# Gate and value products of a gated unit: seven block products per batch in place of full products, with input sums kept in DRAM

## The chip, the cores and the metric

The kernel runs on one core of a Trainium2 chip. The metric is the device time of one execution in microseconds. Before the change, three runs gave a median of 2069.04 us (2067.13 to 2071.77). The execution that the profiler recorded took 2068.53 us; the span from its first to its last instruction is 2066.6 us.

## The reference

Three layers follow each other. A retention layer (4 batches, 8 heads, 576 positions, head width 64) gives x with 2304 tokens and 512 features. A gated unit with 1536 hidden features and then eight dense experts follow:

```python
# gated unit
rms = np.sqrt(np.mean(x * x, axis=-1, keepdims=True) + 1e-06)
xn = x / rms * rms_g
g = xn @ w_gate                      # (2304, 512) @ (512, 1536)
silu = g * (1.0 / (1.0 + np.exp(-g)))
val = xn @ w_val                     # (2304, 512) @ (512, 1536)
x = silu * val @ w_out               # (2304, 1536) @ (1536, 512)
# experts: P is (2304, 8), from x @ w_gate by eight rounds of row and column scaling
for e in range(8):
    out += P[:, e:e+1] * (np.maximum(x @ w1[e], 0) @ w2[e])
```

## The kernel before

Everything is computed in float32 by splitting each operand into a high half (`hi`, rounded to fp32r) and a low half (`lo`, the rest). A product is three matmuls: hi by hi, hi by lo, lo by hi (lines 174 to 176, `products`). Tokens are the moving columns, features lie on the 128 partitions.

The gated unit takes its 1536 hidden features in six sweeps (`NSWEEP`) of two blocks of 128 (`SWEEP`). A sweep goes over all 2304 tokens. The first sweep runs inside the retention stage, in eight blocks of 288 tokens, as soon as a batch of 576 tokens is normed. Sweeps two to six run in the five blocks of

```python
BLOCKS = [(0, 512), (512, 512), (1024, 512), (1536, 384), (1920, 384)]
```

In `gated_block` (line 179 on) a block of a sweep needs, for each of its two m: a gate product `gv` of four k blocks by three matmuls, a value product of the same size, the silu on ScalarE (line 196), the multiplication on VectorE (line 202), and the split of the result into `ghi` (ScalarE, line 203) and `glo` (VectorE, line 204). Then four output products `x` of six matmuls each follow, and VectorE adds each of them to `acc` in SBUF (line 225). Products go to four rotating PSUM banks for `gv` and four for `x`. A block has 72 matmuls, a sweep 360.

The weights come from DRAM as 64-bit words, 512 KB for a block of 128 hidden features of one matrix. They are narrowed to float32 by GpSimd (lines 122 and 130), VectorE (lines 123, 124, 126) and ScalarE (line 127), and split by ScalarE (line 142) and VectorE (line 144). `step_weights` moves these chains on by one step at a time, at places written into the loop, so all engines follow one fixed program order; each engine works its own queue in that order.

The experts behind it already use a seven-block scheme: `block_product` (line 775) takes x and w1 as two by two blocks and needs seven products instead of eight; products run into the single PSUM banks px, py, pz and pv, and ScalarE copies px to py and py to pz to start the next product from a sum (lines 870 and 889). Its first pair of features is `n = 0`.

Every DMA that the change touches goes through the queue of SP, in program order.

Of the kernel before, what the change touches and what calls it, by code (L numbers as in the profile page):

```python
# [23 lines left out]
E = 8  # L24
# [7 lines left out]
BLOCKS = [(0, 512), (512, 512), (1024, 512), (1536, 384), (1920, 384)]  # L32
# [6 lines left out]
PAD = 320  # L39
T = 384  # L40
UNIT = 2 * T
NU = NT // UNIT
# [8 lines left out]
def retention_glu_experts(ctx: ExitStack, tc: tile.TileContext, a, out):  # L51
# [15 lines left out]
    wpool = glu.enter_context(tc.tile_pool(name="wpool", bufs=1, side="right"))  # L67
# [20 lines left out]
    for s in range(NSWEEP):  # L88
        for m in range(s * SWEEP, (s + 1) * SWEEP):
            sources += [a["gate"][m], a["val"][m]]  # L90
        sources += [a["wout"][m] for m in range(s * SWEEP, (s + 1) * SWEEP)]
    raw, raw_of, pieces, slot_of, active = {}, {}, {}, {}, {}
    wslots = wpool.tile([128, NW, 2, 512], F32R, name="wslots")
    pad = wpool.tile([128, PAD // 2], mybir.dt.bfloat16, name="pad")
    slots = [[(wslots[:, i, 0, :], wslots[:, i, 1, :]) for i in range(NW)], []]
    raw_slots = list(range(NRAW))
    n_load, n_next, n_slot, n_done = [0], [0], [0], [0]
# [14 lines left out]
    def narrow_weights(i):  # L112


# [4 lines left out]
        x_f, sign = cv[:, 0, :], cv[:, 1, :]  # L119
        x = x_f.bitcast(I32)  # L120
        least = float(np.array((1023 - 126) << 20, np.int32).view(np.float32))
        nc.gpsimd.tensor_scalar(sign, high_f, -least, None, ALU.is_le)  # L122
        nc.vector.tensor_scalar(x, low, 29, 1 << 30, ALU.logical_shift_right, ALU.bitwise_xor)
        nc.vector.scalar_tensor_tensor(x, high, 3, x, ALU.logical_shift_left, ALU.bitwise_xor)
        yield
        nc.vector.scalar_tensor_tensor(sign, high_f, least, sign, ALU.is_ge, ALU.subtract)
        nc.scalar.activation(x_f, x_f, AF.Abs)
        free_raw(i)
        yield
        nc.gpsimd.tensor_mul(x_f, x_f, sign)  # L130
        yield
        return x_f

    def prepare(i):
        x = yield from narrow_weights(i)
        free = slots[i // (3 * SWEEP) in (2, 4)]
        while i != n_slot[0] or not free:
            yield
        n_slot[0] += 1
        hi, lo = pieces_of = free.pop(0)  # L140
        slot_of[i] = free, pieces_of
# [4 lines left out]

    def step_weights(load=True):
        for i in sorted(active):
            if next(active[i], True):
                del active[i]  # L150
        i = n_next[0]
        if i in raw and len(active) < NCONV:
            active[i] = prepare(i)
            next(active[i])
            n_next[0] += 1
        if load:
            load_weights()
# [6 lines left out]
    def done(n):  # L164
        for _ in range(n):
# [13 lines left out]
    def gated_block(s, t0, n, last, pmm, pac, hp, tp, together, w):  # L179
        p0 = s * 3 * SWEEP  # L180
        g = []
        for m in range(SWEEP):
# [15 lines left out]
            if last:  # L198
                done(2)
# [488 lines left out]
    for _ in first_unit:  # L688
        pass
# [622 lines left out]
```

## Time and profile before

| what | value |
|---|---|
| median of three runs | 2069.04 us |
| profiled execution, its span | 2068.53 us, 2066.6 us |
| first sweep and retention | up to 213 us |
| sweep two | 213 to 296 us |
| sweeps three, four, five | 74.09, 74.09 and 73.99 us |
| sweep six | 518 to about 598 us |
| experts, prepared while their weights are read | 598 to about 1120 us |
| experts, with the weights kept | about 1120 us to the end |
| granted clock over the span | 0.992 |

A row of the profile names the line of the kernel, the engine, the operation, the tile written and the tiles read. PE is the matmul engine, DVE VectorE, ACT ScalarE, POOL GpSimd, SP the queue that issues most DMAs. Matmuls overlap at their ends in the record, so the price of one is read from start to start and not from its duration.

### The profile page before, as it was taken

How to read it: one execution, taken by the hardware profiler on the slowest of the kernel's cores; microseconds unless marked ns; L12 is line 12 of the kernel's file. 1: busy time of each engine (PE TensorE's matmuls, PEld its weight loads, DVE VectorE, ACT ScalarE, POOL GpSimd, SP SyncE). 2: the span in 40 equal slices, each digit the busy share in tenths (PEclk: the TensorE clock that was granted, in tenths of full speed). 3: DMA queues.
4: the chain of work that ended last, by engine and by line, in shares of the span. 5: the costliest groups of instructions: out<-in, count | busy, mean ns of one | idle time of the engine just before them, and what ended most of it. 6: DMA issues, size and time to landing. Idle time of an engine off the chain costs nothing.

```text
span 2066.6 us, 30376 instructions
## 1 busy us (share of the span) xinstructions
PE 2035.1 (98%) x11526; PEld 1883.8 (91%) x11526; DVE 1482.2 (72%) x2324; ACT 862.9 (42%) x1655; POOL 842.9 (41%) x746
## 2 busy tenths in 40 slices
PE   8999999999999999999999999999999999999998
PEld 5688788899788989999998999999999999999998
DVE  6764775653468887777776777777788677777777
ACT  3443331221254454444444544444445544444443
POOL 4411442310024454544561545444455454544443
PEclk8899999999999999999999999999999999999999
DMA  7420221100028888888878767676766676767673
GB/s 233 156 90 1 69 75 41 62 29 3 0 96 306 296 297 299 309 300 306 306 285 329 262 252 275 244 268 247 280 246 260 251 273 252 260 251 281 241 282 138
DMA packets 112690, 436.58 MB, mean 211 GB/s; under 512 B 12297, under 2 KB 30473, under 8 KB 96161
## 3 DMA queue, kind: packets, MB, share of 16 engines
q1 hardware_dynamic: 110048, 432.72, 57.4%
q8 instruction: 90, 1.47, 0.3%
q10 hardware_dynamic: 2496, 1.94, 0.3%
q14 instruction: 56, 0.45, 0.1%
HBM read 312.40 MB, written 122.21 MB: 210 GB/s over the span
## 4 chain that ended last, share of the span: by engine, by line
PE 89%; DVE 6%; ACT 2%; issue 1%; POOL 1%; DMA 1%; ACTq 0%; SPq 0%; DVEq 0%; POOLq 0%
PE pz L775 9%; PE py L775 9%; PE px L775 9%; PE qx L1006 6%; PE qy L1006 6%; PE qz L1006 6%; PE gv L174 5%; PE gv L175 4%; PE gv L176 4%; PE y L175 4%; PE y L176 4%; PE y L174 4%; PE qz L775 3%; PE x L174 2%; PE x L175 2%; PE x L176 2%
## 5 line engine op out<-in xcount | busy, mean ns | idle before, releaser
L1183 POOL TENSOR_TENSOR acc<-z,a_block 128x384 f32<-128x384 f32 x63 | 64.0, 1016 | 446.5 <-DVE z L1177 446.5
L775 PE MATMUL py<-sx,w1s 128*128 128x384 f32 x1152 | 233.0, 336 | 2.8 <-ACT py L1099 2.5
L775 PEld LDWEIGHTS py<-sx,w1s 128*128 128x128 f32 x1152 | 203.5, 188 | 7.2 <-ACT py L1099 4.3
L775 PE MATMUL px<-xhi,w1s 128*128 128x384 f32 x640 | 188.5, 335 | 0.0
L996 ACT CAST xhi<-acc 128x384 fp32r<-128x384 f32 x316 | 156.0, 514 | 69.6 <-POOL acc L1183 35.4
L1000 DVE TENSOR_TENSOR xlo<-acc,xhi 128x384 fp32r<-128x384 f32 x191 | 177.5, 956 | 1.8 <-ACT xhi L996 1.8
L1000 POOL TENSOR_TENSOR xlo<-acc,xhi 128x384 fp32r<-128x384 f32 x125 | 145.4, 1163 | 32.2 <-ACT xhi L996 32.2
L1014 DVE TENSOR_TENSOR acc<-acc,qz 128x384 f32<-128x384 f32 x246 | 134.9, 548 | 26.0 <-PE qz L1006 26.0
L577 POOL TENSOR_TENSOR t<-rw 128x256 f32<-128x256 f32 x32 | 43.0, 1343 | 234.6 <-issue 126.9
L122 POOL TENSOR_SCALAR cv<-raw 128x512 f32<-128x512 f32 x36 | 63.1, 1757 | 182.6 <-DVE wslots L144 91.6
L175 PE MATMUL gv<-xlo,wslots 128*128 128x512 f32 (+2 forms) x368 | 127.4, 346 | 3.0 <-DVE xlo L408 1.7
L174 PE MATMUL gv<-xhi,wslots 128*128 128x512 f32 (+2 forms) x368 | 128.5, 349 | 0.4 <-ACT xhi L405 0.4
L176 PE MATMUL gv<-xhi,wslots 128*128 128x512 f32 (+2 forms) x368 | 126.9, 345 | 0.0
L202 DVE TENSOR_TENSOR t<-t,gv 128x512 f32<-128x512 f32 (+2 forms) x66 | 38.8, 589 | 115.8 <-PE gv L176 115.7
L775 PEld LDWEIGHTS px<-xhi,w1s 128*128 128x128 f32 x640 | 117.9, 188 | 0.3
L1014 DVE TENSOR_TENSOR acc<-acc,qx 128x384 f32<-128x384 f32 x123 | 67.4, 548 | 70.1 <-PE qx L1006 70.1
L775 PE MATMUL pz<-xhi,w1s 128*128 128x384 f32 x384 | 113.8, 337 | 3.2 <-DVE z L930 2.3
L775 PE MATMUL pz<-sx,w1s 128*128 128x384 f32 x576 | 115.6, 335 | 0.0
L775 PE MATMUL px<-xlo,w1s 128*128 128x384 f32 x320 | 106.9, 334 | 0.0
L820 DVE SCALAR_TENSOR_TENSOR acc<-y,prob,acc 128x512 f32<-128x512 f32 x144 | 101.4, 742 | 6.1 <-PE y L176 6.1
L176 PE MATMUL y<-xlo,xhi 128*128 128x512 f32 x264 | 103.9, 393 | 0.0
L175 PE MATMUL y<-xlo,xhi 128*128 128x512 f32 x264 | 103.7, 393 | 0.0
(379 smaller groups left out, 6037.4 us busy)
## 6 DMA issues: line engine op xcount, KB each, us to landing
w1s<-w_kept SPq DMA_DIRECT2D x64, 1792.0 KB, 7.1
w_kept<-w1s SPq DMA_DIRECT2D x32, 1792.0 KB, 6.6
rw<-in_w_dram SPq DMA_DIRECT2D x64, 512.0 KB, 5.5
w_kept<-xlo SPq DMA_DIRECT2D x64, 512.0 KB, 3.7
w2s<-w_kept SPq DMA_DIRECT2D x32, 1024.0 KB, 6.9
w_extra<-w_kept SPq DMA_DIRECT2D x32, 768.0 KB, 7.6
w_kept<-xlo SPq DMA_DIRECT2D x44, 384.0 KB, 4.1
w2c<-w_kept SPq DMA_DIRECT2D x32, 512.0 KB, 7.7
```

Source lines behind the costliest of these rows:

```text
L122: nc.gpsimd.tensor_scalar(sign, high_f, -least, None, ALU.is_le)
L174: nc.tensor.matmul(ps, lhsT=lh, rhs=rh, start=start, stop=False)
L175: nc.tensor.matmul(ps, lhsT=lh, rhs=rl, start=False, stop=False)
L176: nc.tensor.matmul(ps, lhsT=ll, rhs=rh, start=False, stop=stop)
L577: nc.gpsimd.tensor_sub(t[:, 0, :], w[:, 3, :], w[:, 0, :])
L775: nc.tensor.matmul(ps, lhsT=l, rhs=r[:, k, :], start=start and k == 0 and i == 0, stop=k == 1 and i == 2, skip_group_check=True,)
L820: nc.vector.scalar_tensor_tensor(o, y_2, pe, o, ALU.mult, ALU.add)
L996: nc.scalar.copy(hi, x)
L1000: (engine or nc.vector).tensor_sub(lo, x, f32(hi))
L1006: nc.tensor.matmul(ps, lhsT=l, rhs=r, start=start and i == 0, stop=i == 2, skip_group_check=True)
L1014: nc.vector.tensor_add(dst, dst, ps)
L1183: nc.gpsimd.tensor_add(sums[0], z[:, 0, :], h_blocks[0])
```

## The change

For sweeps two to six, gate and value products use the seven-block scheme with batches of 576 tokens as two halves of 288 columns, and 512 features as two halves of 256. The weights of a sweep (two blocks of 128 hidden features) give seven blocks of 256 by 128: four of the original ones and combinations of them, made on GpSimd by four subtractions of 256 columns for each pair of raw blocks. The sums of x (S1 to S4) are made on GpSimd when a batch is normed, split, and stored to DRAM (`x_kept`). S1 is later loaded over the part of `xhi` and `xlo` that is needed no more; S2, S3 and S4 of each batch are loaded again in every sweep into a ring of four places. A unit is one batch in one sweep: a gate half, then a value half, each of seven block products of six matmuls. Between them stand the eight output products (six matmuls of 288 columns each) of the unit before.

The core of the diff:

```diff
-BLOCKS = [(0, 512), (512, 512), (1024, 512), (1536, 384), (1920, 384)]
+HB = S // 2
@@ narrowing, now also for pairs of blocks
+    def pair_of_blocks(at, idx):
...
+        nc.gpsimd.tensor_sub(t0[:, :256], b12, b11)
+        nc.gpsimd.tensor_sub(t0[:, 256:], b22, b12)
+        yield
+        nc.gpsimd.tensor_sub(t1[:, :256], b22, t0[:, :256])
+        nc.gpsimd.tensor_sub(t1[:, 256:], b21, t1[:, :256])
...
+                nc.scalar.copy(r[:, 0, p, :], x)
...
+                nc.vector.tensor_sub(r[:, 1, p, :], x, f32(r[:, 0, p, :]))
@@ after the norm of a batch
+        nc.gpsimd.tensor_add(s1, a21, a22)
+        nc.gpsimd.tensor_sub(s2, s1, a11)
+        nc.gpsimd.tensor_sub(s3, a11, a21)
+        nc.gpsimd.tensor_sub(s4, a12, s2)
+    def split_sums(b, sums):
+        for i, t in enumerate(sums):
+            st = xsums.tile([128, 2, 2, HB], F32R, tag="split", name=f"xsp{b}_{i}")
+            nc.scalar.copy(st[:, 0], t)
+            nc.vector.tensor_sub(st[:, 1], t, f32(st[:, 0]))
+            yield
+            nc.sync.dma_start(x_kept[b][:, i], f32(st).rearrange("p s k t -> p (s k t)"))
@@ the sweeps; gx, gy, gz, gp are px, py, pz, pv with 288 columns
+    def load_sums(used=0):
...
+            t = ring[:, (len(order_of_sums) - 1 - n_sums[0]) % 4]
+            nc.sync.dma_start(f32(t).rearrange("p s k t -> p (s k t)"), x_kept[key[1]][:, key[2]])
...
+            for part in range(2):
...
+                    gated_product(gx, idx, 0, blocks["A11"], start=True)
+                    nc.scalar.copy(gy, gx)
+                    behind()
+                    gated_product(gp, idx, 3, blocks["S1"], start=True)
+                nc.scalar.copy(t[:, 1], gp)
+                between_products(4 * part)
+                gated_product(gy, idx, 4, blocks["S2"])
+                nc.scalar.copy(gz, gy)
...
+                gated_product(gx, idx, 1, blocks["A12"])
+                if part:
+                    nc.vector.tensor_mul(gate_t[:, 0, 0], gate_t[:, 0, 0], gx)
+                    keep_gated(0, 0, n_unit, gate_t[:, 0, 0])
+                else:
+                    nc.scalar.activation(gate_t[:, 0, 0], gx, AF.Silu)
+                between_products(4 * part + 1)
+                gated_product(gy, idx, 2, blocks["S4"])
...
+                nc.vector.tensor_add(t[:, 0], gy, t[:, 1])
+                if part:
+                    nc.vector.tensor_mul(t[:, 0], t[:, 0], gate_t[:, 1, 0])
+                    keep_gated(1, 0, n_unit, t[:, 0])
+                next(ys, None)
+                gated_product(gz, idx, 5, blocks["S3"])
...
+                nc.vector.tensor_add(t[:, 1], gz, t[:, 1])
+                if part:
+                    nc.vector.tensor_mul(t[:, 1], t[:, 1], gate_t[:, 1, 1])
+                    keep_gated(1, 1, n_unit, t[:, 1])
+                else:
+                    nc.scalar.activation(t, t, AF.Silu)
+                between_products(4 * part + 2, False)
+                between_products(4 * part + 3)
+
+                def behind(idx=idx, part=part, x=blocks["A22"], n=n_unit, last=u == B - 1):
+                    gated_product(gz, idx, 6, x)
+                    if part:
+                        nc.vector.tensor_mul(gate_t[:, 0, 1], gate_t[:, 0, 1], gz)
+                        keep_gated(0, 1, n, gate_t[:, 0, 1])
+                    else:
+                        nc.scalar.activation(gate_t[:, 0, 1], gz, AF.Silu)
```

`between_products` issues one output product of the unit before (`ys`) and one step of the weights. `keep_gated` casts on ScalarE and leaves the low half to VectorE, which does it behind the next output product's addition. The logits and the first operands of the experts are taken up in the last sweep at other places, and the first expert pair's second weights are loaded and split at its end rather than at its beginning.

On the matmul engine, at the end of the value products of a block of the fourth sweep, this stood before (gv is a gate or value product, x an output product):

```order
L176 MATMUL gv_1536_1_1_3368<-xhi,sx 128x384
L174 MATMUL x_1536_0_3386<-ghi_1536_0_3348,w1s_2303 128x384 [waits Activation_49]
L175 MATMUL x_1536_0_3386<-glo_1536_0_3349,w1s_2303 128x384 [waits DVE_49]
L176 MATMUL x_1536_0_3386<-ghi_1536_0_3348,w1s_2303 128x384
L174 MATMUL x_1536_1_3387<-ghi_1536_0_3348,w1s_2303 128x384
```

Now, in the value half of the first unit of a sweep, this stands behind the six matmuls of S3 into pz (x is an output product of the unit before, px the product A11 of the next half, pz the product A22 that was left behind):

```order
L255 MATMUL x_0_1_3_4412<-gated,out_w_2061 128x288 [waits DVE_49]
L256 MATMUL x_0_1_3_4412<-gated,out_w_2061 128x288
L257 MATMUL x_0_1_3_4412<-gated,out_w_2061 128x288
L255 MATMUL x_0_1_3_4412<-gated,out_w_2061 128x288
L256 MATMUL x_0_1_3_4412<-gated,out_w_2061 128x288
L257 MATMUL x_0_1_3_4412<-gated,out_w_2061 128x288
L654 MATMUL px<-xhi,wslots 128x288 [waits DVE_49]
L654 MATMUL px<-xlo,wslots 128x288
L654 MATMUL px<-xhi,wslots 128x288 x2
L654 MATMUL px<-xlo,wslots 128x288
L654 MATMUL px<-xhi,wslots 128x288
L654 MATMUL pz<-xhi,wslots 128x288 [waits DVE_49]
```

The product that writes pz again stands two groups of six matmuls behind the product that VectorE has to read from pz; before, a bank was written again after three other products.

On VectorE, at the same block of the fourth sweep, this stood before (t is the gated value, cv a block of weights being narrowed):

```order
L202 TENSOR_TENSOR t_1920_0_3431<-t_1920_0_3431,gv_1920_0_1_3433 128x384 [waits PE_49,Activation_49]
L204 TENSOR_TENSOR glo_1920_0_3447<-t_1920_0_3431,ghi_1920_0_3446 128x384 [waits Activation_49]
L144 TENSOR_TENSOR sx<-cv_3153,sx 128x512 [waits Activation_49]
L144 TENSOR_TENSOR sx<-cv_3210,sx 128x512 [waits Activation_49]
L123 TENSOR_SCALAR cv_3470<-raw_3214 128x512 [waits DMAHW4_49,DVE_49]
L124 SCALAR_TENSOR_TENSOR cv_3470<-raw_3214,cv_3470 128x512 [waits DVE_49]
L202 TENSOR_TENSOR t_1920_1_3466<-t_1920_1_3466,gv_1920_1_1_3474 128x384 [waits PE_49,Activation_49]
L204 TENSOR_TENSOR glo_1920_1_3488<-t_1920_1_3466,ghi_1920_1_3487 128x384 [waits Activation_49]
```

Now, in the value half of a sweep's first unit, from the product that reads px to the addition that reads pz (line 923 is the one for which A22 waits; lines 126 and 127 narrow a block of weights):

```order
L907 TENSOR_TENSOR gate_t<-gate_t,px 128x288 [waits PE_49]
L724 TENSOR_TENSOR acc<-acc,x_0_1_1_4365 128x288 [waits PE_49]
L707 TENSOR_TENSOR gated<-gate_t,gated 128x288 [waits Activation_49]
L126 TENSOR_SCALAR cv_4374<-raw_4155 128x512 [waits DMAHW3_49]
L127 SCALAR_TENSOR_TENSOR cv_4374<-raw_4155,cv_4374 128x512 [waits DVE_49]
L915 TENSOR_TENSOR val_t<-py,val_t 128x288 [waits PE_49]
L917 TENSOR_TENSOR val_t<-val_t,gate_t 128x288 [waits DVE_49]
L724 TENSOR_TENSOR acc<-acc,x_0_1_2_4388 128x288 [waits PE_49]
L707 TENSOR_TENSOR gated<-val_t,gated 128x288 [waits Activation_49]
L923 TENSOR_TENSOR val_t<-pz,val_t 128x288 [waits PE_49]
L925 TENSOR_TENSOR val_t<-val_t,gate_t 128x288 [waits DVE_49]
```

Eight operations, two of them the weights' narrowing, now stand between the read of px (line 907) and the read of pz (line 923); before, five stood between the reads of two value products, and no other product had to wait for the second read until three more had been issued.

## Rows read from the trace of the kernel before

**Rows 1.** The page: span, busy time by engine, and the last chain by engine.
```profile
span 2066.6 us, 30376 instructions
PE 2035.1 (98%) x11526; PEld 1883.8 (91%) x11526; DVE 1482.2 (72%) x2324; ACT 862.9 (42%) x1655; POOL 842.9 (41%) x746
PE 89%; DVE 6%; ACT 2%; issue 1%; POOL 1%; DMA 1%; ACTq 0%; SPq 0%; DVEq 0%; POOLq 0%
```
**Rows 2.** Stretches: length, busy time and instructions by engine, clock, DMA share, GB/s.
```profile
core 0: us, PE busy (x) PEld busy (x) DVE busy (x) ACT busy (x) POOL busy (x), PEclk, DMA share, GB/s
295.90:344.90 49.00, 49.00 (x217) 40.56 (x217) 33.56 (x46) 12.33 (x21) 16.75 (x11) 1.00 0.21 65
344.90:369.99 25.09, 25.09 (x145) 24.96 (x144) 11.48 (x21) 5.51 (x11) 3.40 (x2) 1.00 0.00 1
295.90:369.99 74.09, 74.09 (x361) 65.52 (x361) 45.04 (x66) 17.84 (x32) 20.15 (x13) 1.00 0.14 43
212.98:295.90 82.92, 78.92 (x386) 68.45 (x385) 64.65 (x90) 26.96 (x50) 38.40 (x25) 1.00 0.25 77
70.00:213.00 143.00, 137.79 (x1145) 117.20 (x1146) 81.05 (x174) 60.20 (x131) 30.23 (x21) 0.95 0.20 65
807.70:823.27 15.57, 15.57 (x80) 14.08 (x79) 11.42 (x16) 6.73 (x10) 7.90 (x9) 1.00 0.84 303
```
**Rows 3.** Matmuls of 288 columns in the first sweep: start, duration, engine, line.
```profile
196.56 0.40 PE L174 MATMUL x<-ghi,wslots 128*128 128x288 f32 x1
...
198.25 0.29 PE L174 MATMUL gv<-xhi,wslots 128*128 128x288 f32 x1
...
204.59 0.29 PE L174 MATMUL x<-ghi,wslots 128*128 128x288 f32 x1
...
206.43 0.40 PE L174 MATMUL x<-ghi,wslots 128*128 128x288 f32 x1
```
**Rows 4.** Waits of PE, 213 to 620 us.
```profile
PE x L176 <- DVE wslots L144: 2.4, 1, 2.4
PE x L174 <- ACT wslots L142: 1.3, 1, 1.3
```
**Rows 5.** VectorE by line and shape, 60 to 620 us: busy, mean ns, idle before.
```profile
L225 DVE TENSOR_TENSOR acc<-acc,x 128x512 f32<-128x512 f32 x60 | 40.7, 687 | 18.7 <-PE x L176 18.7
L126 DVE SCALAR_TENSOR_TENSOR cv<-raw,cv 128x512 f32<-128x512 f32 x30 | 31.5, 1051 | 0.4 <-POOL cv L122 0.4
L124 DVE SCALAR_TENSOR_TENSOR cv<-raw,cv 128x512 int32<-128x512 int32 x29 | 27.2, 938 | 1.0
L123 DVE TENSOR_SCALAR cv<-raw 128x512 int32<-128x512 int32 x29 | 20.2, 696 | 0.4
L144 DVE TENSOR_TENSOR wslots<-cv,wslots 128x512 fp32r<-128x512 f32 x19 | 12.9, 686 | 0.2
L204 DVE TENSOR_TENSOR glo<-t,ghi 128x288 fp32r<-128x288 f32 x16 | 7.3, 459 | 8.0 <-ACT ghi L203 8.0
L202 DVE TENSOR_TENSOR t<-t,gv 128x288 f32<-128x288 f32 x16 | 7.2, 452 | 20.5 <-PE gv L176 20.5
L410 DVE TENSOR_TENSOR xlo<-acc,xhi 128x576 fp32r<-128x576 f32 x4 | 3.0, 752 | 0.1
```
**Rows 6.** ScalarE and GpSimd by line and shape, 60 to 620 us.
```profile
L223 ACT COPY acc<-x 128x288 f32<-128x288 f32 x32 | 12.3, 399 | 9.9 <-PE x L176 9.7
L405 ACT CAST xhi<-acc 128x576 fp32r<-128x576 f32 x16 | 10.8, 675 | 12.1 <-DVE acc L404 11.9
L366 POOL TENSOR_TENSOR sq<-sq,sq 128x576 f32<-128x576 f32 x9 | 13.9, 1544 | 68.0 <-ACT sq L364 40.4 <-issue 27.6
L408 POOL TENSOR_TENSOR xlo<-acc,xhi 128x576 fp32r<-128x576 f32 x4 | 7.7, 1928 | 11.4 <-ACT xhi L405 11.4
```
**Rows 7.** Timeline: start, duration, engine, line; a low half on VectorE, twice.
```profile
74.02 1.78 POOL L130 TENSOR_TENSOR cv<-cv 128x512 f32<-128x512 f32 x1
...
74.60 1.82 DVE L408 TENSOR_TENSOR xlo<-acc,xhi 128x576 fp32r<-128x576 f32 x1
...
107.28 0.75 DVE L408 TENSOR_TENSOR xlo<-acc,xhi 128x576 fp32r<-128x576 f32 x1
```
**Rows 8.** SP's waits, 70 to 213 us, and a weights' DMA: KB, us to landing.
```profile
SPq L279 <- PE ot L350: 44.2, 7, 8.1
raw<-in_wout_dram SPq DMA_DIRECT2D x9, 512.0 KB, 3.5
```
**Rows 9.** The last chain in the first expert pair, 598 to 620 us.
```profile
602.14 1.23 DVE xlo L748
611.16 0.95 ACT w1s L587
```

More of the change, by code (lines that the diff above doesn't have):

```diff
@@ new lines, in out_blocks @@
+    def out_blocks(at, s):
+        while at not in raw:
+            yield
+        one = narrow_bits(at)
+        yield
+        while at + 1 not in raw:
+            yield
+        two = narrow_bits(at + 1)
+        yield
+        narrow_sign(at, *one)
+        narrow_product(one[0])
+        yield
+        narrow_sign(at + 1, *two)
+        narrow_product(two[0])
+        yield
+        while len(out_slots) < 2:
+            yield
+        homes = [out_slots.pop(0) for _ in range(2)]
+        for (hi, lo), c in zip(homes, (one, two)):
+            nc.scalar.copy(hi, c[0][:, 0, :])
+            yield
+            nc.vector.tensor_sub(lo, c[0][:, 0, :], f32(hi))
+        out_pieces[s] = homes
+        yield
@@ L367, in outputs, with split_step @@
         squares[b] = sq
-    normed = set()
+    normed, splits, stored, first_done = set(), [], set(), set()
+    x_kept = [kept.tile([128, 4, 4 * HB], F32, tag=f"xs{b}", name=f"x_kept{b}") for b in range(B)]
+    def split_sums(b, sums):
[3 more added lines that the diff above has]
+            nc.vector.tensor_sub(st[:, 1], t, f32(st[:, 0]))
+            yield
+            nc.sync.dma_start(x_kept[b][:, i], f32(st).rearrange("p s k t -> p (s k t)"))
+            if i == len(sums) - 1:
+                stored.add(b)
+            yield
+    def split_step():
+        if splits and next(splits[0], True):
+            splits.pop(0)
     def norm(b):
@@ new lines, in retention_glu_experts, with gated_product @@
+    while splits:
+        split_step()
+    assert len(first_done) == 2 * B
+    free_regions.add(1)
+    def gated_product(ps, idx, w, x, start=False):
+        while idx not in ready_pairs:
+            step_weights()
+        r = regions[idx % 3]
+        xh, xl = x
+        for k in range(2):
+            kc = slice(k * 128, (k + 1) * 128)
+            wh, wl = r[:, 0, w, kc], r[:, 1, w, kc]
+            for i, (l, m) in enumerate(((wh, xh), (wh, xl), (wl, xh))):
+                nc.tensor.matmul(
+                    ps, lhsT=l, rhs=m[:, k, :], start=start and k == 0 and i == 0,
+                    stop=k == 1 and i == 2, skip_group_check=True,
+                )
@@ L696, in retention_glu_experts @@
+    next(scored)
+    behind()
+    assert next(stream, None) is None and n_load[0] == len(sources) and not raw
     slabs = [x[:, k, UNIT:] for x in (xhi, xlo) for k in range(KD)]
@@ L870, in retention_glu_experts @@
         nc.scalar.copy(py, px)
+        if not n:
+            flush()
+            next(scored)
+            load_job2(0)
         if n == 1:
@@ L932, in retention_glu_experts @@
         if not n:
-            between(n)
+            next(scored)
             next(weights)
```

453 lines of the change are left out of this document (282 added, 171 removed).

## The prediction

> **What bounds the kernel now.** I read the page first. PE is busy for 98% of the span, and the last chain is PE for 89% of it [rows 1]. Then the stretches. Sweep three lasts 74.09 us and PE is busy for all of it; VectorE is busy for 45.04 us, ScalarE for 17.84, GpSimd for 20.15 [rows 2]. So in sweeps three to five only the number and the length of matmuls count. Sweep two takes 82.92 us and begins with two waits for weights, 2.4 and 1.3 us [rows 4]. The granted clock is 1.00 in all these stretches (the 2.4 GHz level), so the clock is no term here.
>
> A matmul's price is its distance from start to start. With 512 columns it is 49.00 us / 216 = 226.9 ns, with 384 columns 25.09 / 144 = 174.2 ns [rows 2]; the one matmul more in each count there overlaps the edge of the stretch. The first sweep shows 288 columns: 48 matmuls from 198.25 to 204.59 us, 132.1 ns each; over 72 matmuls with their hand-overs between banks, 196.56 to 206.43, 137.1 ns [rows 3].
>
> **Part 1, the matmuls: -21.7 us.** A sweep has 360 matmuls now, for 74.09 us. The change issues per unit 2 halves x 7 products x 6, and 8 output products x 6: 132 matmuls of 288 columns, 528 in a sweep. At 132.1 ns that is 69.74 us. The gain is 74.09 - 69.74 = 4.35 us a sweep, 21.7 in five. At 137.1 ns it is 72.39 us, a gain of 8.5 in five; this is my other end. I take 132.1, since the expert pairs, built of the same single banks, keep PE busy for 15.57 of 15.57 us with VectorE at 11.42 [rows 2].
>
> By the Trainium skill (TensorE: Matmul & The Clock Gate, section Back-to-back issue gap) a matmul takes some 81 ns at 128 columns and 131 ns at 512, so that most of its price is fixed; by a straight line between these the 528 short ones would cost 53.9 us against 44.7 for the 360 long ones, an estimate from that page, and each sweep would lose 9 us. The trace disagrees: 226.9, 174.2 and 132.1 ns grow almost with the columns, so that way gets no chance below.
>
> **Part 2, waits of PE inside a sweep: +12.5 us.** VectorE gets more, shorter work. Per unit there are 4 additions from PSUM, 4 multiplications, 4 low halves and 8 additions to acc, 20 operations of 288 columns at 452 to 459 ns [rows 5], 9.1 us. Per sweep that is 36.4. Weights add six times (696 + 938 + 1051) ns = 16.1 us and the low halves of 14 blocks of 256 and two of 512, about 6.3 by the 686 ns of 512 columns [rows 5]. Together 58.8 of 69.74 us, 84%: it fits, but not at every place.
>
> The tight place is in the value half. A22 of the half writes pz again two groups of six matmuls (2 x 0.793 us) after S3, and waits until VectorE has read S3. Ahead of that read stand operations which I count for each of a sweep's four units, from the addition after the fourth group of the half, which can begin when that group ends. Eight groups, 6.34 us, lie between that moment and A22.
> - Unit one: nine short ones (4.08 us) and two blocks' first two narrowing steps (2 x 1.634): 7.35 us. Late by 1.0, with about 0.3 for hand-overs 1.3 us.
> - Unit two: nine short, one such step pair and one sign step (1.051): 6.76 us. Late by 0.4, with hand-overs 0.7.
> - Unit three: behind the seventh group (five groups, 3.97 us, to A22) two short ones, two low halves of weights (1.1) and five short: about 4.3 us. Late by 0.3, with hand-overs 0.5.
> - Unit four has its heavy step before the read of px and is in time.
>
> That is 2.5 us a sweep, 12.5 in five. What stands behind A22 on PE is everything; VectorE's own later work only gains from the pause. Lower end 0 (as in the expert pairs). Upper end: below, with the rival on VectorE. ScalarE has 6 PSUM copies a unit at about 399 ns [rows 6], with two groups or more (1.59 us) to do each; weights' casts that wait for GpSimd stand between them. I price it at nothing beside VectorE; if a cast is late by a group, it costs 0.8 us each time.
>
> The ring of sums: a place is freed in the value half and needed 13 groups (10.3 us) later. 590 KB at the 3.5 us of 512 KB land in about 4 us [rows 8], which leaves 6 us for what SP has to wait for in front of it: hidden.
>
> **Part 3, opening of sweep two: -2.5 us.** Before, sweep two's 82.92 us hold 74.09 of matmuls and 24 of the first sweep's tail (3.2): 5.6 us are lost, 3.7 of them in [rows 4]. These waits go. Late next: the first unit has no output products between its own, so S3 to A22 is one group (0.79 us) for an addition of 0.45 and a hand-over, S2 to S4 one group for a copy of 0.40; and the value weights are split while it runs. I take 3.1 us for that, between 0 and 8.
>
> **Part 4, the stage before: +1.5 us.** The norm adds 16 sums on GpSimd (1.54 to 1.93 us each, 25 to 31 us to 30.23 busy in 143), 16 casts on ScalarE (675 ns, 10.8 us to 60.20) and 16 low halves on VectorE (752 ns, 12 us to 81.05) [rows 2, 5, 6]. There is room. But all splits use one staging tile: a cast waits until the last store has landed, that store stands on SP behind loads which wait for PE for up to 8.1 us [rows 8], and ScalarE waits with its queue. I take 1.5 us, between 0 and 9 (nine such casts late by 1 us).
>
> **Part 5, the passage to the experts: +0.5 us.** The first pairs run on chains of VectorE, ScalarE and GpSimd, such as the weights' splits of 1.23 and 0.95 us [rows 9]. First weights and operands now come earlier, but eight output products of a batch, two more logit steps and the second weights come later. Between -3 and +5.
>
> **Sum.** -21.7 + 12.5 - 2.5 + 1.5 + 0.5 = -9.7 us from the profiled execution's 2068.5 us (0.5 below the median of the runs): 2059 us.
>
> **Rivals.**
> - The waits are hidden. The expert pairs with VectorE at 73% speak for it, the higher share of 84% and the shorter groups against. Without part 2: 2068.5 - 21.7 - 0.5 = 2046 us.
> - VectorE becomes the bound, and the kernel slower. Line 408 on VectorE takes 0.75 us alone, but 1.82 us beside a multiplication on GpSimd that runs from 74.02 to 75.80 us: it ends 0.62 us behind it [rows 7]. The change adds 8 subtractions on GpSimd per sweep, to 12 operations there. If each holds a VectorE operation up by 1.1 us, and half of them in a value half that is late already, a sweep takes 69.74 + 2.5 + 4.4 = 76.6 us, 2.6 more than now, so +13 in five: 2068.5 + 13 - 0.5 = 2081 us. It decides from 4.35 us of waits a sweep on. Against it: the means of [rows 5] hold such collisions already. The Trainium skill (GPSIMD Engine Reference, section Key points) says that GpSimd shares its SBUF interfaces with VectorE and contends with VectorE instructions of two SBUF inputs; line 408 is one, and the trace agrees by its 1.82 us. No row here shows how often it will meet.
> - Short matmuls cost their hand-overs: 137.1 ns each, a gain of 8.5 in place of 21.7: 2072 us. For it the 72 matmuls of [rows 3], against it the expert pairs without idle time.
> - The early stage and the passage are both at their dear ends (+7.5 and +4.5): 2059 + 12 = 2071 us.
>
> **How the numbers follow.** Forecast 0.50 (its own range 2050 to 2068), waits hidden 0.17, VectorE bound 0.13, early stage and passage 0.12, dear matmuls 0.08. A measurement of this kernel can tell 0.2%, 4.1 us, so faster is below 2064.9 and slower above 2073.2. Of the forecast 0.38 lies in faster and 0.11 in between; with all of the hidden case and a few hundredths of the last two, faster is 0.62; between is 0.19; slower has most of the VectorE case and the tails, 0.19. The range 2045 to 2076 leaves out the VectorE case and little below.
>
> **What would show it.** PE: 2640 matmuls of 288 columns in five sweeps, 132 ns apart, in place of 1800. A sweep of 70 to 73 us. PE's waits list VectorE's read of pz (line 923) as the longest of the new ones, some 15 times, most in the first unit of each sweep. VectorE busy at 80 to 85% of a sweep. Sweeps of 74 us or more, waits for the ring's DMA, or line 923 absent from the waits would show my account wrong; so would more than 215 us before the first product of sweep two.

## The result and the profile after

The changed kernel takes 2083.89 us (median of four runs, 2079.56 to 2088.70). The kernel before, run beside it, takes 2068.09 us. The ratio is 1.0074 (95% interval 1.0046 to 1.0102): slower by 15.8 us, where 9.7 us of gain were forecast. The profiled execution took 2079.56 us, the fastest of the four; granted clocks over the span were 0.992, 0.987, 0.991 and 0.985, and the slower the run, the lower its clock.

The page of the changed kernel answers to [rows 1]: span, busy time by engine, the last chain by engine.

```profile
span 2077.8 us, 32776 instructions
PE 2023.3 (97%) x12374; PEld 1909.7 (92%) x12374; DVE 1547.2 (74%) x2553; ACT 926.4 (45%) x1849; POOL 907.6 (44%) x806
PE 81%; DVE 10%; ACT 3%; DMA 1%; issue 1%; POOL 1%; ACTq 0%; SPq 0%; DVEq 0%; POOLq 0%
```

PE is busy for 11.8 us less and the span is 11.2 us longer: 23 us more stand idle. The chain says who ends last there: PE's share falls from 89 to 81%, VectorE's rises from 6 to 10%.

The stretches answer to [rows 2]: length, busy time and count by engine (PE, its weight loads, VectorE, ScalarE, GpSimd), granted clock, DMA share, GB/s. First 70 us to the first product of sweep two; then its last part, from the matmul `rb` of batch four's norm on; then one sweep, from VectorE's line 907 in the first unit of one sweep to the same place in the next.

```profile
70.00:229.30 159.30, 141.52 (x1135) 119.46 (x1135) 111.85 (x203) 69.75 (x151) 70.45 (x51) 0.95 0.43 151
181.20:229.30 48.10, 38.42 (x234) 35.40 (x235) 29.72 (x45) 21.38 (x48) 23.76 (x17) 0.89 0.51 181
351.38:423.62 72.24, 70.88 (x530) 69.95 (x529) 52.50 (x109) 29.07 (x68) 24.22 (x20) 1.00 0.46 143
```

The same last part of the first stage, in the kernel before:

```profile
178.85:212.98 34.13, 32.49 (x235) 30.94 (x233) 13.47 (x24) 14.37 (x34) 2.55 (x2) 1.00 0.01 1
```

A sweep takes 72.24 us in place of 74.09: that part works. The first product of sweep two comes at 229.3 us in place of 212.98, and 14.0 of these 16.3 us arise in the last part, with the same 235 matmuls. PE is idle there for 48.10 - 38.42 = 9.7 us (1.6 before), and is busy for 5.9 us more at a granted clock of 0.89 instead of 1.00. From the first product of sweep two to the end of the span the changed kernel is 5.1 us faster (1848.5 against 1853.6).

What PE waits for in that last part: line and tile, releaser, us in total, times, longest.

```profile
PE x L255 <- ACT acc L299: 4.1, 2, 2.6
PE gv L255 <- DVE t L280: 2.4, 1, 2.4
PE gv L255 <- ACT t L276: 1.5, 2, 1.2
PE x L255 <- ACT ghi L281: 1.3, 1, 1.3
```

All are hand-overs of the first sweep that existed before, when PE waited at one of them only (178.85 to 213 us):

```profile
PE x L174 <- ACT acc L223: 1.5, 1, 1.5
```

Now other work stands in front of them on ScalarE and VectorE. The timeline shows some pieces: start, duration, engine, line.

```profile
199.31 3.16 SPq L635 DMA_DIRECT2D gated<-x_kept  x6
...
202.57 0.66 SPq L448 DMA_DIRECT2D x_kept<-xsp  x1
203.51 0.63 ACT L133 ACTIVATE cv<-cv 128x512 f32<-128x512 f32 x1 [1.78 <-DVE cv L127]
204.04 0.68 ACT L299 COPY acc<-x 128x288 f32<-128x288 f32 x2
204.48 0.61 PE L255 MATMUL x<-ghi,wslots 128*128 128x288 f32 x1 [2.64 <-ACT acc L299]
...
209.65 0.67 ACT L445 CAST xsp<-xs 128x576 fp32r<-128x576 f32 x1 [4.39 <-DMA x_kept<-xsp]
...
210.35 0.76 DVE L446 TENSOR_TENSOR xsp<-xs,xsp 128x576 fp32r<-128x576 f32 x1 [4.67 <-ACT xsp L445]
...
212.90 0.44 DVE L280 TENSOR_TENSOR t<-t,gv 128x288 f32<-128x288 f32 x1
...
213.40 0.40 PE L255 MATMUL gv<-xhi,wslots 128*128 128x288 f32 x1 [2.43 <-DVE t L280]
...
215.82 0.67 ACT L445 CAST xsp<-xs 128x576 fp32r<-128x576 f32 x1 [2.02 <-DMA x_kept<-xsp]
...
216.40 0.40 ACT L276 ACTIVATE t<-gv 128x288 f32<-128x288 f32 x1
...
216.86 0.61 PE L255 MATMUL gv<-xhi,wslots 128*128 128x288 f32 x1 [1.20 <-ACT t L276]
```

ScalarE waits 1.78 us for a step of the weights (line 133), so its copy for PE (line 299) is late and PE waits 2.64 us. Later a cast into the staging tile waits 4.39 us for a store that was issued behind six loads; the low half of the sum on VectorE (line 446) waits for that cast, line 280 stands behind it, and PE waits 2.43 us for line 280. The next cast waits 2.02 us for its store, with the silu (line 276) behind it, and PE waits 1.20 us.

The price of a matmul, as in [rows 3]; the three rows are the same place in three half units.

```profile
377.82 0.29 PE L654 MATMUL px<-xhi,wslots 128*128 128x288 f32 x1
...
386.55 0.29 PE L654 MATMUL px<-xhi,wslots 128*128 128x288 f32 x1
...
395.28 0.29 PE L654 MATMUL px<-xhi,wslots 128*128 128x288 f32 x1
```

132 matmuls lie between the first and the last: 17.46 us / 132 = 132.3 ns.

PE's waits from sweep two to 620 us, against [rows 4], and the stretches around the largest two:

```profile
PE pz L654 <- DVE val_t L923: 3.8, 8, 0.8
PE lg L740 <- ACT xhi L728: 3.4, 1, 3.4
PE lg L740 <- DVE xlo L707: 3.0, 2, 2.7
PE py L654 <- ACT pz L902: 1.9, 5, 0.4
```

```profile
590.00:595.00 5.00, 4.08 (x31) 3.71 (x29) 4.28 (x7) 1.77 (x3) 3.85 (x4) 1.00 0.00 0
595.00:600.00 5.00, 1.10 (x3) 0.25 (x3) 3.70 (x8) 1.59 (x3) 0.00 (x0) 0.69 0.00 0
600.00:605.00 5.00, 3.41 (x12) 2.66 (x13) 1.96 (x5) 1.14 (x2) 0.00 (x0) 0.50 0.00 0
605.00:610.00 5.00, 5.00 (x28) 4.52 (x28) 1.27 (x5) 1.52 (x4) 0.00 (x0) 0.79 0.31 105
610.00:615.00 5.00, 5.00 (x35) 5.00 (x34) 2.45 (x6) 2.12 (x4) 0.00 (x0) 1.00 0.02 5
```

The second hole is new: the logits of block four (line 740) stop PE for 6.4 us in front of the experts. The clock falls to the lower level (0.50, 1.2 GHz) after PE has idled and is back at 1.00 after 610 us. Six matmuls of 288 columns from 603.03 to 604.47 us take 240 ns each in place of 132.3:

```profile
603.03 0.44 PE L654 MATMUL pz<-xhi,w1s 128*128 128x288 f32 x1
...
604.47 0.52 PE L1028 MATMUL px<-xhi,wslots 128*128 128x384 f32 x1
```

The Trainium skill (Perfetto Trace Analysis, section Matmul Optimizations) says that the matmul engine scales power with its use and that matmuls should be executed back to back. The rows show the clock and not the power; they agree in that the clock fell after PE had idled.

### The profile page after: what moved, and what is told of

It is laid out like the page before. It is cut to its first block, busy times and chain, and to the rows that moved or that the text cites. A ratio compares the mean times of both kernels' runs of the same rounds, so it can differ in the third digit from the quotient of the medians.

```text
span 2077.8 us, 32776 instructions
## 1 busy us (share of the span) xinstructions
PE 2023.3 (97%) x12374; PEld 1909.7 (92%) x12374; DVE 1547.2 (74%) x2553; ACT 926.4 (45%) x1849; POOL 907.6 (44%) x806
## 4 chain that ended last, share of the span: by engine, by line
PE 81%; DVE 10%; ACT 3%; DMA 1%; issue 1%; POOL 1%; ACTq 0%; SPq 0%; DVEq 0%; POOLq 0%
PE pz L1028 9%; PE py L1028 9%; PE px L1028 9%; PE qy L1260 6%; PE qx L1260 6%; PE qz L1260 6%; PE y L256 4%; PE y L257 4%; PE y L255 4%; PE qz L1028 3%; PE pz L654 2%; PE py L654 2%; PE px L654 2%; PE x L255 2%; PE x L257 2%; PE x L256 2%
## 5 line engine op out<-in xcount | busy, mean ns | idle before, releaser
L724 DVE TENSOR_TENSOR acc<-acc,x 128x288 f32<-128x288 f32 x160 | 72.0, 450 | 73.6 <-PE x L257 73.4
L1005 POOL TENSOR_TENSOR t<-rw 128x256 f32<-128x256 f32 x32 | 42.2, 1318 | 154.3 <-DVE xlo L1014 110.1
L1286 ACT COPY qz<-qy 128x384 f32<-128x384 f32 x127 | 58.8, 463 | 106.8 <-PE qy L1260 99.4
L783 POOL TENSOR_TENSOR t<-rw 128x256 f32<-128x256 f32 x32 | 44.4, 1389 | 136.3 <-DMA rw<-in_w_dram 57.2
L257 PE MATMUL y<-xlo,xhi 128*128 128x512 f32 x264 | 103.9, 393 | 0.0
L256 PE MATMUL y<-xlo,xhi 128*128 128x512 f32 x264 | 103.7, 393 | 0.0
L255 PE MATMUL y<-xlo,xhi 128*128 128x512 f32 x264 | 102.8, 389 | 0.0
L1278 ACT COPY qy<-qx 128x384 f32<-128x384 f32 x127 | 58.8, 463 | 95.8 <-PE qx L1260 89.4
L1028 PE MATMUL px<-xhi,wslots 128*128 128x384 f32 x320 | 94.9, 337 | 0.0
L256 PE MATMUL x<-gated,out_w 128*128 128x288 f32 x320 | 94.1, 294 | 0.9 <-DVE gated L707 0.8
L1028 PE MATMUL px<-xhi,w1s 128*128 128x384 f32 x320 | 94.4, 335 | 0.0
L255 PE MATMUL x<-gated,out_w 128*128 128x288 f32 x320 | 94.3, 295 | 0.0
L257 PE MATMUL x<-gated,out_w 128*128 128x288 f32 x320 | 94.1, 294 | 0.0
L137 POOL TENSOR_TENSOR cv<-cv 128x512 f32<-128x512 f32 x36 | 49.0, 1366 | 98.6 <-DVE cv L132 47.8
```

The lines of the kernel that those rows point to most:

```text
L255: nc.tensor.matmul(ps, lhsT=lh, rhs=rh, start=start, stop=False)
L256: nc.tensor.matmul(ps, lhsT=lh, rhs=rl, start=False, stop=False)
L257: nc.tensor.matmul(ps, lhsT=ll, rhs=rh, start=False, stop=stop)
L724: nc.vector.tensor_add(acc_d[:, d, tokens], acc_d[:, d, tokens], y)
L1028: nc.tensor.matmul(ps, lhsT=l, rhs=r[:, k, :], start=start and k == 0 and i == 0, stop=k == 1 and i == 2, skip_group_check=True,)
```

## The experiments

Each kernel ran in five rounds beside the kernel before, whose median was 2067.2 to 2067.6 us. The four runs of the changed kernel spread over 9 us, so a difference to its median of 2083.89 us is known to about 6 us either way (95%); the intervals in the table are 1.8 to 3.7 us either way.

| label | us | ratio to before (95%) |
|---|---|---|
| late_loads | 2081.09 | 1.0056 (1.0043 to 1.0069) |
| no_staging | 2066.78 | 0.9991 (0.9982 to 1.0001) |
| before_sums | 2088.28 | 1.0091 (1.0073 to 1.0109) |
| late_logits | 2087.08 | 1.0091 (1.0079 to 1.0104) |
| sums_no_split | 2070.95 | 1.0014 (1.0005 to 1.0022) |
| split_no_store | 2079.61 | 1.0057 (1.0045 to 1.0069) |
| ns_one_step | 2062.02 | 0.9967 (0.9954 to 0.9980) |
| spread_operands | 2086.36 | 1.0090 (1.0076 to 1.0104) |
| one_late | 2075.88 | 1.0042 (1.0028 to 1.0056) |
| one_late_pool | 2084.02 | 1.0076 (1.0064 to 1.0088) |
| one_late_pool_spread | 2077.97 | 1.0048 (1.0036 to 1.0060) |
| no_operands | 2076.24 | 1.0039 (1.0026 to 1.0052) |
| one_late_spread | 2074.31 | 1.0028 (1.0018 to 1.0038) |
| ols_low_pool | 2073.89 | 1.0031 (1.0021 to 1.0042) |
| ols_cast_pool | 2084.51 | 1.0074 (1.0062 to 1.0086) |
| ols_value_step | 2070.41 | 1.0013 (1.0003 to 1.0024) |
| best_low | 2070.30 | 1.0014 (1.0004 to 1.0024) |
| best_later | 2070.13 | 1.0009 (1.0000 to 1.0018) |

**The loads moved behind the last store.**

```diff
+        if len(stored) == B:
+            if not kept_first: keep_first_sum(0)
+            elif homes: ...   # one sum's two loads per step
```

> The loads of the stored sums into their first homes and over the first block are issued one at a time, and only after the last store of batch four. Theory (the staging tile): in the changed kernel a cast into the one staging tile waits 4.39 and 2.02 us for the store before it, which lies in the DMA queues behind eight loads (DMA share 1.00 at 200 to 210 us); ScalarE's copies for PE stand behind that cast, and PE then falls to the low clock. Without loads in front of the stores the first product of sweep two starts at 216 to 220 us instead of 229.3, and the whole is 9 to 13 us shorter, about 2070 to 2074 us. Rival one (the work of the sums, casts and low halves itself fills the engines) and rival two (two steps of weights per step of the loop): the start stays at 227 to 230 us, the whole within 3 us of 2084.

The theory fell, and the rivals' numbers held. The casts' waits for the store in the last part went from 6.9 to 0.2 us, but the total by only 2.8 us, which is within the scatter of the changed kernel. Its last part of the first stage, `rb` to first product, was still this long:

```profile
183.67:229.29 45.62, 37.59 (x234) 34.55 (x235) 32.21 (x45) 21.52 (x48) 24.15 (x17) 0.93 0.44 159
```

**No sums at all, and the sums alone.**

```diff
-        s1, s2, s3, s4 = (xsums.tile(...) ...)   # and the four sums, casts, low halves
+                nc.sync.dma_start(x_kept[b][:, i, ...], f32(x[:, 2:4, b * S:b * S + HB]))
```

> The sums, their casts and their low halves are left out (the stores take other data straight from xhi and xlo, so the numbers stored are not the sums); stores, loads and weights' steps stay. Theory of the staging tile: no cast waits for a store any more, the first product of sweep two starts at 215 to 219 us, the whole at 2068 to 2073 us. Rival one (work of the sums) expects the same here. Rival two (weights' steps in the loop, two per step): start at 225 us or later, the whole within 4 us of 2084.

The same stretch of no_staging, from `rb` of batch four to the first product of sweep two:

```profile
173.23:215.90 42.67, 36.04 (x237) 33.84 (x236) 23.53 (x39) 18.38 (x42) 17.70 (x13) 0.92 0.58 188
```

17.1 us less than the changed kernel, with start at 215.90. Theory and rival one expected much the same here, so this run does not tell them apart. `rb` of batch four comes 8.0 us earlier than in the changed kernel; executions of the same instructions differ by 3.5 us there (last section). The stretch is still 42.67 us long.

The kernel before, with the lines of sums, casts, low halves and stores put in:

> The kernel before with the sums, splits and stores alone added to its first stage, and no load of them. Theory of the staging tile behind loads: no loads, so the casts wait little; the first product of sweep two comes at 214 to 217 us (212.98 without the sums) and the whole is 1 to 4 us over before. Rival one (work of the sums): 222 us or later, 10 us or more over before. Rival two (weights' steps): 0 to 2 us over before.

Rival one held: 20.9 us over the kernel before in the median, with nothing else of the change. In the profiled execution the first product of sweep two comes at 228.06 in place of 212.98 us, and what is left of the span lasts 1854.2 us (1853.6 before): there the whole price lies in the first stage. PE's longest waits, 60 to 232 us, are hand-overs behind ScalarE's queue:

```profile
PE u L327 <- ACT ks L290: 3.6, 1, 3.6
PE x L174 <- ACT acc L223: 3.4, 2, 1.9
```

**The sums taken apart.**

```diff
# sums_no_split: no cast, no low half, no staging
-            st = xsums.tile(...); nc.scalar.copy(st[:, 0], t); nc.vector.tensor_sub(st[:, 1], ...)
+            for j in range(2): nc.sync.dma_start(x_kept[b][:, i, ...], t)
# split_no_store: staging as it was, stores from elsewhere
-            nc.sync.dma_start(x_kept[b][:, i], f32(st)...)
+            nc.sync.dma_start(x_kept[b][:, i, ...], f32(x[:, 2:4, b * S:b * S + HB]))
```

> The sums on GpSimd stay, but they are stored as they are, twice, straight from their four tiles: casts, low halves and the staging tile are left out (what is loaded as high and low half is the sum itself, so the output is not the reference's). The kernel without sums took 2066.8 us, the changed one 2083.9. Theory now (staging): the 17 us come from the casts and low halves that wait in ScalarE's and VectorE's order, so without them 2066 to 2071 us, first product of sweep two at 215 to 220 us. Rival (GpSimd's sums): norms late because GpSimd is full and holds up VectorE, 2078 to 2084 us, first product at 224 or later.

> Sums, casts and low halves into the one staging tile stay; the stores take other data straight from xhi and xlo (so the numbers loaded are not the sums), and no cast waits for a store. Theory that the wait for the store is the price: 2066 to 2072 us, as without staging. Rival (the work itself, in the engines' order, 16 casts of 0.67 us and 16 low halves of 0.75 us): 2079 us or more, and PE's waits for acc and t in 181 to 229 us stay at 6 us or more.

So the 17.1 us are three steps: the sums on GpSimd 2070.95 - 2066.78 = 4.2, casts and low halves 2079.61 - 2070.95 = 8.7, stores ahead of casts 2083.89 - 2079.61 = 4.3. The rival of split_no_store held in time: casts and low halves are the largest part, clear of noise (9.0 us by the means, 7.4 to 10.6); so are the 4.2 us of the sums. The 4.3 us of the stores are within the scatter of the changed kernel. PE's waits for acc and t in split_no_store came to 5.1 us, below the 6 expected, with 3.7 more for `ghi`.

The same last part of sums_no_split and of split_no_store:

```profile
176.71:220.30 43.59, 37.19 (x236) 34.54 (x235) 27.57 (x40) 18.34 (x42) 24.01 (x17) 0.92 0.56 185
182.75:228.81 46.06, 37.49 (x234) 34.54 (x235) 32.28 (x45) 21.28 (x48) 24.36 (x17) 0.93 0.54 175
```

Casts and low halves lengthen it by only 2.5 us in these two executions; the other 6.0 us arise ahead of `rb` of batch four, with the batches before.

**One step of weights in the dense loop.**

```diff
         next(dense)
         step_weights()
         split_step()
-        step_weights()
```

> As the kernel without sums (no_staging, 2066.8 us, first product of sweep two at 215.90, PE's waits in 190 to 210 us of 5.9 and granted clock 0.50 at 205 to 210), with one step of weights instead of two in each step of the dense loop. Theory: the hole left there comes from the weights' steps that ScalarE and VectorE run between the hand-overs; with half of them the first product starts at 211 to 213 us; some weights then come later and cost 1 to 4 us in sweep two; whole 2062 to 2067 us. Rival (the loads of the sums, DMA share 0.97 and 0.81 in 190 to 210 us, make the hole): start stays at 215 to 217 us.

The same stretch of ns_one_step:

```profile
178.25:212.72 34.47, 32.83 (x237) 31.30 (x236) 23.06 (x37) 17.30 (x40) 10.91 (x7) 1.00 0.61 203
```

The stretch fell from 42.67 to 34.47 us, the length before the change, and the clock stayed at 1.00, with the DMA share as high as in no_staging (0.97 in 190 to 210 us): without the second step the loads don't stop PE. So the second step is the largest piece of the 14.0 us of the last part. But `rb` came 5.0 us later here, so the first product of sweep two was only 3.2 us earlier, at 212.72, and PE then waited 1.8 us for weights in sweep two. In the total 4.8 us stayed by the medians; the two profiled executions took the same time (2066.4 and 2066.0 us).

> The changed kernel with the loads of the sums after the last store (late_loads, 2081.1 us) and one step of weights instead of two in each step of the dense loop (4.8 us where there were no sums: 2066.8 to 2062.0). Theory that both prices add: 2075 to 2078 us, first product of sweep two at 223 to 226 us. Rival: the casts and low halves alone hold PE up there, so the weights' steps are hidden behind them: 2080 us or more.

The same stretch of one_late:

```profile
182.48:222.09 39.61, 34.79 (x234) 31.65 (x235) 27.85 (x42) 20.02 (x46) 17.60 (x11) 1.00 0.38 141
```

The theory's total held, 5.2 us under late_loads by the medians (3.7 by the means, which is just clear of noise); the first product came at 222.09, 0.9 us ahead of the forecast. What is left over the 34.13 us of before goes with the sums and their splits, since it is gone without them (34.47 in ns_one_step).

**The hole in front of the experts.** Block four's logits moved behind the first expert product; then two operand splits moved there as well.

```diff
-    next(scored)
     behind()
# spread_operands, in addition
-            if spot not in (1, 2): next(first_unit, None)
+            if spot in (0, 3, 4): next(first_unit)
# ... the other two behind the products A11 and S1 of the first pair
```

> The logits of the fourth block (1152 to 1535) are issued behind the first product of the experts instead of in front of the last gated product, the later ones one place later each. Theory: in the changed kernel PE does 2.2 us of work between 593.75 and 604.47 us, the rest waits for xlo and xhi of that block (2.74 and 3.38 us) and runs at a granted clock of 0.50 to 0.69; with the place moved the wait is covered by 1.6 to 3 us of products and the clock holds, so the whole is 6 to 9 us shorter, 2075 to 2078 us. Rival: VectorE is late with everything there (val_t, acc, xlo in its order), so the wait only moves to the gated product or the first pair, and the whole is within 2 us of 2084.

PE's longest waits in late_logits, 590 to 640 us:

```profile
PE pz L654 <- DVE val_t L923: 3.6, 1, 3.6
PE pz L1027 <- DVE z L1179: 2.3, 1, 2.3
```

> The logits of block four are issued behind the first product of the experts, and two of the four splits of the first experts' operands (0.83 us on ScalarE, 0.96 to 1.49 us on VectorE each) are taken out of the last unit's value half and issued behind the first two products of the experts. Theory: late_logits moved the wait to VectorE's read of pz (3.65 us) since VectorE was late by those splits; with two of them gone the wait at 594 to 602 us falls from 8.5 us lost to 1 to 3 and the clock stays at 1.00; whole 2076 to 2079 us. Rival: the backlog goes with the splits into the first pair, where S3 or S4 wait for them: within 2 us of 2084 to 2087.

Both theories fell. Both rivals held in what they name: PE waits for VectorE a product later, and the last logits, later by one place too, stop it again (1.3 and 1.1 us in spread_operands); late_logits lies 3.2 us over the changed kernel, where within 2 was expected, inside the scatter. Leaving the splits out names the cause:

> The changed kernel with the four splits of the first experts' operands left out (S1 to S4 of the first 768 tokens are then stale data, so the output is not the reference's). Theory: these splits in the last unit's value half make VectorE late there and open the hole of 593.75 to 604.47 us; without them the hole falls from 8.5 us lost to 2 or less, the clock stays at 1.00, and the whole is 2073 to 2077 us. Rival (the logits wait for the last units' own output products, wherever VectorE stands): 2081 us or more, and the waits of PE for xlo and xhi of block four stay at 4 us or more.

PE's waits in no_operands, 580 to 620 us:

```profile
PE lg L740 <- ACT xhi L728: 1.3, 1, 1.3
PE pz L1024 <- DVE z L1176: 1.2, 1, 1.2
PE lg L740 <- DVE xlo L707: 0.4, 1, 0.4
```

The 6.4 us for block four are down to 1.7, and the granted clock stays at 1.00 from 590 to 610 us. The theory held, 7.7 us under the changed kernel (with the 6 us of scatter either way; the hole itself was 8.5 us). GpSimd is idle from 590 to 610 us in this run, so its collisions with VectorE there (last section) are gone too.

**Other engines for the splits.** First cast and low half on GpSimd, then one of the two.

```diff
-            nc.scalar.copy(st[:, 0], t)
+            nc.gpsimd.tensor_copy(st[:, 0], t)      # one_late_pool, ols_cast_pool
-            nc.vector.tensor_sub(st[:, 1], t, f32(st[:, 0]))
+            nc.gpsimd.tensor_sub(st[:, 1], ...)     # one_late_pool, ols_low_pool
```

> As one_late, and the cast and the low half of every sum run on GpSimd instead of ScalarE and VectorE. Theory: it is the place in ScalarE's and VectorE's order that costs 8.7 us (split_no_store against sums_no_split), GpSimd has room (it is busy for 74 of 170 us at 60 to 230 us): 2066 to 2070 us. Rival (GpSimd as the next late one, and VectorE slowed beside it as in [rows 7]): the norms' xlo, sq and the weights' products wait for GpSimd, 2075 us or more.

> As one_late_pool, and two of the four splits of the first experts' operands are issued behind the first two products of the experts, with the logits of block four left in their place. Theory: the wait for block four (xlo 2.74 us, xhi 3.38 us) is VectorE's lateness by those splits, so it falls to 2 us or less: 3 to 6 us below one_late_pool. Rival (the experts' first pair takes the wait over, as in spread_operands): within 2 us of one_late_pool.

> one_late (2075.9 us) with two of the four splits of the first experts' operands issued behind the first two products of the experts, logits in their place. Theory that the prices add: 6 us less (one_late_pool to one_late_pool_spread: 2084.0 to 2078.0), so 2068 to 2072 us, no slower than before by more than 4 us. Rival: the first pair takes the wait over, 2074 to 2077 us.

> one_late_spread with the low halves of the sums on GpSimd, the casts still on ScalarE. If VectorE's order is what the splits cost: 3 to 6 us below one_late_spread. If it is ScalarE's order: the same within 2 us, or dearer, since the staging tile then waits for a slower low half (GpSimd takes 1.4 to 1.9 us for 576 columns, VectorE 0.75). With both moved GpSimd was 8 us dearer.

> one_late_spread with the casts of the sums on GpSimd, the low halves still on VectorE. If ScalarE's order is what the splits cost (its queue holds the copies and casts PE waits for): 3 to 6 us below one_late_spread. If GpSimd's slowness decides, as when both were moved: 4 us or more above it, since VectorE then waits in its order for a cast of 1.4 us or more on GpSimd, behind the norm's operations there.

GpSimd is no way out. Both there cost 8.1 us over one_late, against the theory; the cast alone costs 10.2 us over one_late_spread, the low half changes nothing (-0.4). So these runs don't tell ScalarE's share of the 8.7 us from VectorE's: each move also makes the staging chain slower. Two operand splits moved behind the first products gave 6.0 us on one_late_pool, but only 1.6 on one_late, where 6 were expected. The rival's number came, but not its mechanism: PE's waits for block four fell from 6.8 to 3.3 us and the first pair waits no more than before (1.2 us). In the profiles the first stage of one_late_spread is 3.6 us later than that of one_late (225.7 against 222.09) with the same instructions up to there, so the first stage scatters by as much.

**The order inside a sweep.**

```diff
+                if spot != 5:
                     step_weights()
...
                     keep_gated(1, 1, n_unit, t[:, 1])
+                    step_weights()
```

> one_late_spread with one step of weights of each value half moved from in front of VectorE's read of pz (line 923) to behind it. The sweeps last 72.23 us, 528 matmuls at 132.5 ns are 69.96, so 2.27 us a sweep are waits. Theory of the prediction (the steps ahead of that read are what makes it late): waits for line 923 vanish, a sweep lasts 71.0 to 71.7 us, the whole is 3 to 6 us below one_late_spread. Rival: the step makes the next read late instead (line 935 or the next unit's), sweep 72 us or more, whole within 2 us.

One sweep of ols_value_step, from line 907 of one first unit to the next:

```profile
349.60:420.65 71.05, 70.16 (x530) 69.92 (x529) 51.93 (x109) 29.10 (x68) 24.04 (x20) 1.00 0.46 145
```

A sweep lasts 71.05 us, 1.2 less, and line 923 is gone from PE's waits. The total fell by 3.9 us in the medians (2.6 in the means), less than five times 1.2: PE's waits for ScalarE's copy of py (3.3 us, 1.6 in one_late_spread) and for the low halves of the gated values (3.0 us, 0.8) grew.

**All together.**

> ols_value_step (2070.4 us) with the low halves of the sums on GpSimd, as in ols_low_pool. By the sums of the parts: 0 to 1 us below ols_value_step, 2069 to 2071 us, still within 0.2% of before. Rival (GpSimd later, VectorE earlier, with the first stage's norms 3 to 6 us earlier as the one profile of ols_low_pool has them): 2065 to 2068 us.

> best_low with the split of the third operand (S2) too moved behind the last gated product, so none but the first stays in the last unit. Theory: the waits in front of the experts (5.5 us in ols_value_step) fall to 2 us or less: 2 to 4 us below best_low. Rival: S2's product is the third of the first pair, 3.7 us behind, and waits for the split; the same within 2 us of best_low.

Both stay at 2070 us, so best_low's first expectation and best_later's rival held. They are 0.14 and 0.09% over the kernel before, with intervals of 0.04 to 0.24% and 0.00 to 0.18%: no faster, and slower by hardly more than can be told. No version found that keeps the sums beats the kernel before.

## Why the prediction was wrong

- **Part 1, matmuls: right.** 132.3 ns measured, 132.1 taken.
- **Part 2, waits inside a sweep: right in size, and half of it shown.** 528 x 132.3 ns = 69.85 us, so 72.24 us hold 2.4 us of waits (2.5 forecast). One step moved from in front of line 923 takes 1.2 us of them away (ols_value_step). But PE's waits name line 923 only 8 times, not 15, with 3.8 us of the 12 in five sweeps; 1.9 us go to ScalarE's copy (line 902), which was priced at nothing, and what holds the rest is not shown. That the size came out to 0.1 us a sweep is in part luck. VectorE's operations were counted well: their durations add up to 57.6 us in the sweep shown (58.8 forecast). They overlap at their ends in the record, so VectorE is busy for 52.50 us, 73%, not 84%.
- **Part 3, opening: right, even low.** 229.30 to 243.30 us hold 93 matmuls, 12.3 us, so 1.7 us are lost up to there instead of 3.1.
- **Part 4, the stage before: the step that failed.** "There is room" compared the added work with idle time per engine. The first sweep there is a chain of hand-overs between PE, ScalarE and VectorE, and each engine runs in its order. The sums, splits and stores cost 17.1 us (no_staging; 20.9 in before_sums), against 1.5 forecast and 9 as the upper end. The mechanism named, the wait for the store, does stop PE (2.43 and 1.20 us in the rows above), but it is the smaller part: 4.3 us by split_no_store, 2.8 by late_loads, neither clear of noise. That the casts and low halves cost 8.7 us is shown. That they do so by their place in front of what PE waits for fits the rows, but no run shows it apart from the work itself.
- **Part 4 left out a moved piece.** The dense loop takes two steps of weights where it took one, and the steps now find work: even with one of them and no sums VectorE is busy for 23.06 us of that stretch, 13.47 before. With one the stretch is as short as before (34.47 us), so it is the second that stops PE, though VectorE is hardly busier with it (23.53 us). It costs 4.8 to 5.2 us by the medians (ns_one_step, one_late). Part 3 credited the end of the waits for weights and did not charge the place to which this work went.
- **Part 5, passage: the other size that failed.** Operands were said to "come earlier". Their splits stand in the last unit, ahead of reads by VectorE and casts by ScalarE for which PE waits: 7.7 us (no_operands) against 0.5, and 5 as the upper end.
- **The sum.** Sweeps -9.25 (five times 1.85), opening -3.9, sums +17.1, second step +4.8, operands +7.7: +16.5 us, against 15.8 measured. The closeness is in part luck: in the profiled execution the first stage is 16.3 us longer, not 17.1 + 4.8 = 21.9, so these prices partly cover one another or scatter. By that execution alone, +16.3 for the first stage and -13.15 for sweeps and opening leave +8.0 for the passage and what follows, 11.2 us together.
- **The rivals.** "Early stage and passage both dear" named the right places, with upper ends too small (9 for 17.1 us, 5 for 7.7). "VectorE becomes the bound" gave 2081 us, near the result, by the wrong way: sweeps last 72.24, not 76.6 us. The sign that the prediction set, over 215 us before the first product of sweep two, came true.

## What to carry to other kernels

Price work added to a stage of tight hand-overs by where it stands in each engine's order: what is queued behind it, and which of that does PE wait for. A share of idle time did not give the price here: ScalarE was idle for 58% and VectorE for 43% of the first stage before (from 70 us on), and casts and low halves cost 8.7 us. When a wait for weights is taken out of one place, charge the place where their preparation runs instead; and count PE's time after a gap at the clock that the rows beside such gaps show.

## What was not expected of the hardware

A gap costs more than itself. In the last part of the first stage 8.0 us more of idle time came with 5.9 us more of busy time for the same 235 matmuls. Executions of the same instructions differ in it: `rb` of batch four began at 181.19 us in the changed kernel and at 184.71 in late_logits, which is the same up to there. In 90 to 100 us the granted clock was 1.00 in the one and 0.50 in the other; in the 5 us ahead PE had been busy for 5.00 us in the one and 3.59 in the other.

VectorE beside GpSimd, as in [rows 7], met the first experts' splits too (start, duration, engine, line):

```profile
586.73 0.96 DVE L823 TENSOR_TENSOR xlo<-s,xhi 128x768 fp32r<-128x768 f32 x1 [0.55 <-ACT xhi L822]
587.83 1.85 POOL L835 TENSOR_TENSOR s<-acc 128x768 f32<-128x768 f32 x1 [18.96 <-DVE xlo L823]
...
588.77 1.53 DVE L707 TENSOR_TENSOR xlo<-acc,xhi 128x576 fp32r<-128x576 f32 x1
...
590.22 1.49 DVE L823 TENSOR_TENSOR wslots<-acc,wslots 128x768 fp32r<-128x768 f32 x1
```

Line 823 takes 0.96 us alone and 1.49 us beside GpSimd's subtractions, line 707 1.53 us beside line 835. The Trainium skill (GPSIMD Engine Reference, section Key points) says that GpSimd contends with VectorE instructions of two SBUF inputs; the rows agree, and here it fell on the unit in which PE waited for VectorE.
